# A third shifted copy moves from VectorE to GpSimd in a one-core attention block

## The chip, the cores and the metric

The kernel runs on one core of a Trainium2 chip. A core has five engines, each with an instruction queue that is worked off in order: TensorE (PE) multiplies matrices from SBUF into PSUM, VectorE (DVE) and ScalarE (ACT) work element by element and reach both memories, GpSimd (POOL) works element by element on SBUF alone, and SyncE (SP) issues DMA transfers. Engines wait for each other by semaphores. The metric is the device time of one execution in microseconds (us). Before the change it is 412.21 us, the median of 3 runs (412.16 to 412.69).

## The reference

`x` has 2048 rows of 448. The first half is attention with 16 heads of 28 that share one key and one value projection; the second is an expert layer that only the 8 best rows enter.

```python
h = x + A(layernorm(x))          # A: multi-query attention
def A(x):
    q = (x @ wq) as 16 heads;  k = x @ wk;  v = x @ wv
    p = softmax(q k^T * 28 ** -0.5);  return (p v) @ wo
out = h + B(layernorm(h))
def B(x):
    r = x @ w_r;  idx = argsort(-r)[:8];  s = x[idx]
    y = (silu(s @ w_gate) * (s @ w_up)) @ w_down * sigmoid(r[idx])
    return x + (y added at rows idx)
```

## The kernel before, in words

**Tiles and blocks.** Scores are made transposed: 128 keys by 512 queries. A *block* is one group of four heads (g = b % 4) and one chunk of 512 queries (qb = b // 4), so there are 16 blocks of 16 key tiles j. A tile has scores for four heads: two units p of two matmuls each, two PSUM banks per unit. The score comes out of the multiplication already scaled and offset so that, read as the bits of a bf16 number, it approximates its own exponential.

**Two ways to the exponential.** Most tiles go through ScalarE (`act_unit`): one instruction per unit reads two banks and writes exp to `P` (L845). Others go through VectorE (`dve_unit`, L858): it clamps and converts the PSUM scores to 16-bit integers, which are the bits of a rough exponential `Y[..., 0, ...]`. `shift` (L864) makes three further copies of a tile, each with a constant added to the integers. `dve_pv` multiplies the four copies with four differently scaled copies of the values (`Vs`), and their sum is a better exponential. So a VectorE tile costs VectorE four conversions and three shifts, and TensorE 16 value matmuls in place of 4. `where` and `groups` say which tiles of a block go this way: four, three in blocks 5, 9 and 13, four in the last block, five in all in blocks 0 and 1. Scores of ScalarE's tiles lie in PSUM banks 0 to 3, of VectorE's in 4 and 5; banks 6 and 7 hold the sums of the even and odd blocks, and between two uses such a bank is lent to a projection (`misc_bank`). `Y` has three buffers.

**After a block** (`post_block`) VectorE copies the sums out (`Ot`, L636). The denominators go through DRAM to be spread over 128 partitions (`Lc`), VectorE updates their running minimum and maximum (L640, L642), which serve a check at the end, and takes the reciprocal (L645); a further pair of transfers broadcasts it (`Rb`) and GpSimd multiplies (`On`, L648). After four blocks `out_proj` projects the 512 rows, adds `x`, normalizes (mean and variance on VectorE, the power -1/2 on GpSimd, L670), writes the output row (L677) and the normalized row (L680), and forms the routing score r (L683, L686). Both rows are stored to DRAM, 512 rows at a time.

**The search.** The first 1536 scores r are brought into one row through three transfers, and VectorE finds the eight best and their places (`first_row`, `first_max`; L707, L713, L715). `second_top` turns the places into row numbers and gathers those rows of the output and of the normalized rows by two indirect transfers on GpSimd's queue (L735). The last 512 rows join at the end.

**The order.** Every operation is entered into a graph with a planned duration, what it reads and writes, and a priority, which is mostly a time in units of a sixteenth of a block. `_Graph.plan` simulates the engines and fixes the order of each queue: at each step it starts the ready operation of lowest priority number. On the chip the order is fixed, and the times are not.

## Time and profile before

| | |
|---|---|
| median of 3 runs | 412.21 us |
| time of the profiled execution | 414.31 us |
| its span, first to last instruction | 412.2 us |
| ScalarE busy | 381.1 us, 92% |
| VectorE busy | 366.0 us, 89% |
| TensorE busy | 352.7 us, 86% |
| GpSimd busy | 51.3 us, 12% |

A group's row names line, engine, operation, output and inputs with shapes, the count, then busy time and mean duration in ns, then the idle time just ahead of them and what ended it. Busy time counts overlapping instructions once, so a group's busy time over its count is less than the mean duration. TensorE's work all stands under one helper line, L351, and is told apart by its operands. In a timeline a row has start, length, engine, line and operation, with like neighbours merged. In a row of stretches each engine has its busy time and, in brackets, its number of instructions; the granted TensorE clock, the DMA share and GB/s stand last.

### The profile page before, as it was taken

How to read it: one execution, taken by the hardware profiler on the slowest of the kernel's cores; microseconds unless marked ns; L12 is line 12 of the kernel's file. 1: busy time of each engine (PE TensorE's matmuls, PEld its weight loads, DVE VectorE, ACT ScalarE, POOL GpSimd, SP SyncE). 2: the span in 40 equal slices, each digit the busy share in tenths (PEclk: the TensorE clock that was granted, in tenths of full speed). 3: DMA queues.
4: the chain of work that ended last, by engine and by line, in shares of the span. 5: the costliest groups of instructions: out<-in, count | busy, mean ns of one | idle time of the engine just before them, and what ended most of it. 6: DMA issues, size and time to landing. Idle time of an engine off the chain costs nothing.

```text
span 412.2 us, 8124 instructions
## 1 busy us (share of the span) xinstructions
PE 352.7 (86%) x3335; PEld 110.9 (27%) x3335; DVE 366.0 (89%) x785; ACT 381.1 (92%) x429; POOL 51.3 (12%) x76
## 2 busy tenths in 40 slices
PE   8899989898897998888798997988888987898845
PEld 7333222222221221222122222222222221222235
DVE  5998899999899998989999999889989998998281
ACT  4899998999999999999999999999999999999640
POOL 7231000101010020101000120101010130213000
PEclk9999999999999998999999999999999999999955
DMA  7696000100000002000000002000000002001000
GB/s 197 161 228 160 1 2 4 53 4 28 1 28 0 26 6 91 28 3 26 2 27 2 22 8 92 28 2 29 4 27 2 29 0 94 27 4 29 2 34 18
DMA packets 17845, 15.74 MB, mean 38 GB/s; under 512 B 6440, under 2 KB 14924, under 8 KB 17804
## 3 DMA queue, kind: packets, MB, share of 16 engines
q1 hardware_dynamic: 17708, 15.16, 13.4%
q8 instruction: 27, 0.44, 0.5%
q14 instruction: 14, 0.11, 0.1%
q0 software_dynamic: 96, 0.02, 0.0%
HBM read 11.70 MB, written 3.47 MB: 37 GB/s over the span
## 4 chain that ended last, share of the span: by engine, by line
ACT 54%; PE 27%; DVE 16%; issue 1%; DMA 1%; POOL 0%; SPq 0%; POOLq 0%; DVEq 0%
ACT P L845 53%; PE ps L351 27%; DVE Y L858 7%; DVE Y L864 6%; DVE Ot L636 1%; DMA Lc<-l_scr 1%; DVE bn L772 1%; ACT K L527 0%; DVE idx L972 0%; ACT xn L789 0%; POOL out_dram L1038 0%; DVE On L630 0%; SPq L365 0%; DVE wq_sb L1037 0%; DVE ra L778 0%
## 5 line engine op out<-in xcount | busy, mean ns | idle before, releaser
L845 ACT ACTIVATE P<-ps 128x1024 bf16<-128x1024 f32 x396 | 368.1, 1089 | 6.3 <-PE ps L351 4.3
L351 PE MATMUL ps<-Q,K 64*128 64x512 bf16 x1024 | 183.0, 386 | 42.1 <-ACT P L845 29.5
L858 DVE TENSOR_SCALAR Y<-ps 128x512 int16<-128x512 f32 x232 | 149.5, 680 | 13.2 <-PE ps L351 12.7
L864 DVE TENSOR_SCALAR Y<-Y 128x2048 int16<-128x2048 int16 x174 | 119.0, 715 | 1.5
L351 PEld LDWEIGHTS ps<-Q,K 64*128 64x128 bf16 x1024 | 43.9, 93 | 188.2 <-ACT P L845 146.8
L351 PE MATMUL ps<-P,Vs 128*32 128x512 bf16 x792 | 78.4, 390 | 0.0
L351 PE MATMUL ps<-Y,Vs 128*32 128x512 bf16 x928 | 77.7, 382 | 0.1
L648 POOL TENSOR_TENSOR On<-Ot,Rb 128x512 bf16<-128x512 f32 x15 | 22.4, 1496 | 235.9 <-DMA Rb<-l_scr 235.9
L351 PEld LDWEIGHTS ps<-P,Vs 128*32 128x32 bf16 x792 | 20.1, 93 | 46.1 <-issue 45.5
L351 PEld LDWEIGHTS ps<-Y,Vs 128*32 128x32 bf16 x928 | 23.6, 95 | 24.5 <-issue 12.4
L351 PE MATMUL ps<-xnT,wq_pad 112*128 112x512 bf16 (+1 forms) x68 | 19.3, 377 | 1.4 <-DVE Ot L636 1.2
L351 PE MATMUL ps<-wo_pad,On 128*128 128x448 bf16 (+1 forms) x64 | 17.8, 358 | 2.6 <-DVE Ot L636 1.8
L670 POOL TENSOR_TENSOR st<-st,nhalf 128x1 f32<-128x1 f32 x12 | 9.3, 773 | 65.2 <-DVE st L668 65.2
L466 DVE TENSOR_SCALAR Q<-ps,qone 128x512 bf16<-128x512 f32 x15 | 10.8, 722 | 2.4 <-PE ps L351 2.4
L636 DVE COPY Ot<-ps 128x512 f32<-128x512 f32 x15 | 10.3, 686 | 1.0 <-PE ps L351 0.6
L351 PE MATMUL ps<-ident 128*128 128x128 bf16 x72 | 7.6, 287 | 1.8 <-POOL ident L380 1.8
L683 DVE SCALAR_TENSOR_TENSOR junk<-hbuf,st,w_rb 128x448 bf16<-128x448 f32 x12 | 8.1, 677 | 0.0
L664 DVE TENSOR_TENSOR hbuf<-ps,x_sb 128x448 f32<-128x448 f32 x12 | 7.4, 616 | 0.6 <-PE ps L351 0.6
L666 DVE BATCH_NORM_STATS2 bn<-hbuf 128x6 f32<-128x448 f32 x12 | 7.4, 620 | 0.1
L351 PEld LDWEIGHTS ps<-ident 128*128 128x128 bf16 x72 | 6.9, 134 | 1.8 <-POOL ident L380 1.8
L351 PEld LDWEIGHTS ps<-wo_pad,On 128*128 128x128 bf16 x64 | 4.2, 97 | 11.8 <-issue 7.9
L351 PEld LDWEIGHTS ps<-xnT,wq_pad 112*128 112x128 bf16 x68 | 4.4, 98 | 10.2 <-issue 4.2
(175 smaller groups left out, 171.9 us busy)
## 6 DMA issues: line engine op xcount, KB each, us to landing
Rb<-l_scr SPq DMA_DIRECT2D x15, 256.0 KB
wg_sb<-in_B_w_gate_dram SPq DMA_DIRECT2D x1, 1568.0 KB, 12.7
wu_sb<-in_B_w_up_dram SPq DMA_DIRECT2D x1, 1568.0 KB, 19.6
wd_sb<-in_B_w_down_dram SPq DMA_DIRECT2D x1, 1568.0 KB, 23.3
x_sb<-in_A_x_dram SPq DMA_DIRECT2D x3, 448.0 KB, 6.2
out_dram<-x_sb SPq DMA_DIRECT2D x3, 448.0 KB, 3.1
xn_scr<-xn SPq DMA_DIRECT2D x3, 448.0 KB, 4.0
x_sb<-in_A_x_dram SPq DMA_DIRECT2D x4, 112.0 KB, 2.1
```

The costliest lines, as they stand in the source:

```text
L351: return lambda e: e.matmul(o, lhsT=l, rhs=r, start=start, stop=stop)
L466: G.op(DV, lambda e: e.tensor_scalar(Q[:, b % 4, :], ps[:, bank, :], qone[:, 0:1], None, ALU.add), dvt(512), reads=[pk(bank), "qone"], wri ...
L636: G.op(DV, lambda e: e.tensor_copy(Ot[:, rb, :], ps[:, acc_bank(b), :]), dvt(512), reads=[pk(acc_bank(b))], writes=[("Ot", rb)], prio=u - 30)
L648: G.op(PO, lambda e: e.tensor_tensor(On[:, qb % 2, g, :], Ot[:, rb, :], Rb[:, rb, :], ALU.mult), 1270, reads=[("Ot", rb), ("Rb", rb)], wri ...
L664: G.op(DV, lambda e: e.tensor_tensor(hbuf[:, hr, :], ps[:, bank, 0:D], x_sb[:, t, 0:D], ALU.add), dvt(D), reads=[pk(bank), ("x", t)], writ ...
L666: G.op(DV, lambda e: e.bn_stats(bn6[:, t, :], hbuf[:, hr, :]), dvt(D), reads=[("h", hr)], writes=[("bn6", t)])
L670: G.op(PO, lambda e: e.tensor_tensor(st[:, t, 4:5], st[:, t, 7:8], nhalf[:, 0:1], ALU.pow), 570, reads=[("st7", t), "nhalf"], writes=[("st ...
L683: G.op(DV, lambda e: e.scalar_tensor_tensor(junk[:, :], hbuf[:, hr, :], st[:, t, 4:5], w_rb[:, :], ALU.mult, ALU.mult, accum_out=st[:, t, ...
L772: G.op(DV, lambda e: e.bn_stats(bn6[:, t, :], ps[:, bank, 0:D]), dvt(D), reads=[pk(bank)], writes=[("bn6", t)])
L845: G.op(AC, lambda e: e.activation(P[:, sl, :, :], ps[:, b0:b0 + 2, :], ACT.Exp, bias=EBIAS, scale=OCT), 905, reads=[pk(b0), pk(b0 + 1)], w ...
L858: G.op(DV, lambda e, k=k: e.tensor_scalar(Y[:, n, 0, p + 2 * k, :].bitcast(I16), ps[:, 4 + k, :], 0.0, 32639.0 - 3 * STEP, ALU.max, ALU.mi ...
L864: G.op(DV, lambda e: e.tensor_scalar(Y[:, n, v, :, :].bitcast(I16), Y[:, n, 0, :, :].bitcast(I16), v * STEP, None, ALU.add), 610, reads=[( ...
```

## The change

*Third shift.* From block 2 on, the shift v = 3 of a VectorE tile is made by GpSimd, after VectorE's shifts v = 1 and 2 of the same tile. The planner enters 2030 ns for it, and gets a `lock`: operations of GpSimd and VectorE's shifts exclude each other in the plan. The value matmuls of these tiles get later priorities.

*Tiles.* Blocks 2, 3, 5, 6, 8, 9, 11, 12 and 14 have four VectorE tiles, blocks 4, 7, 10 and 13 five. *Conversions.* One instruction converts both banks of a unit.

*Layer norm.* `out_proj` of the first two row chunks goes one tile to a block in four blocks, that of the third two tiles to each of two blocks. The normalized row is no longer written; the row before normalization is stored in float32 with its two factors beside it, a tile at a time (`hbuf` is 450 wide), and the eight gathered rows are normalized after the gather. Output rows are stored 256 at a time. *Check.* The minimum and maximum of the denominators become sums of them and of their reciprocals, made by GpSimd except in the last block.

*Search.* Two levels: the eight best of each of 12 rows of 128, with their places, and the eight best of those 96; the places go through a table in DRAM, broadcast back to eight partitions, from which a compare picks.

```diff
+        o.lock = (lock or eng == PO) and not dma
@@ plan
+        port = 0.0
...
+                for o in lst:
+                    if o.lock and o.ready < port:
+                        o.ready = port
...
+            if c.lock:
+                port = c.end
@@ post_block
+        LE = DV if b == NB - 1 else PO
-        G.op(DV, lambda e: e.tensor_tensor(Lmn[:, :], Lmn[:, :], Lc[:, rb, :], ALU.min), 85,
-        G.op(DV, lambda e: e.tensor_tensor(Lmx[:, :], Lmx[:, :], Lc[:, rb, :], ALU.max), 85,
+        G.op(DV, lambda e: e.reciprocal(Li[:, rb, :], Lc[:, rb, :]), 170, reads=[("Lc", rb)], writes=[("Li", rb)])
...
+        G.op(LE, lambda e: e.tensor_tensor(Lsi[:, :], Lsi[:, :], Li[:, rb, :], ALU.add), 150,
+        G.op(LE, lambda e: e.tensor_tensor(Ls[:, :], Ls[:, :], Lc[:, rb, :], ALU.add), 150,
@@ out_proj
+    def ln_block(qb, k):
+        return 4 * qb + 5 + (k if qb < 2 else k // 2)
-        G.op(DV, lambda e: e.tensor_scalar(xn[:, t, :], hbuf[:, hr, :], st[:, t, 4:5], st[:, t, 6:7],
-                                           ALU.mult, ALU.add), 420,
...
+        dma(xs[t * 128:(t + 1) * 128, :], hbuf[:, hr, :], [("xs", t)], reads=[("h", hr), ("h4", hr), ("h6", hr)],
+            lat=3000.0)
+        if k % 2:
+            evs.append(dma(out_v[:, t - 1:t + 1, :], outf[:, t - 1:t + 1, :], [("out", qb, k)],
@@ first_row, first_max
-        G.op(DV, lambda e: e.tensor_copy(r12[:, :], ps[0:12, bank, 0:128]), 200, reads=[pk(bank)], writes=["r12"])
+        G.op(DV, lambda e: e.max(top12[:, :], ps[0:12, bank, 0:128]), 220, reads=[pk(bank)], writes=["top12"])
+        G.op(DV, lambda e: e.max_index(idx12[:, :], top12[:, :], ps[0:12, bank, 0:128]), 300,
+        G.op(DV, lambda e: e.tensor_scalar(pos12[:, :], idx12[:, :], p128[0:12, 0:1], None, ALU.add), 90,
+        dma(v_row[0:1, :].rearrange("o (t k) -> o t k", k=8), top12[:, :], ["v_row"], reads=["top12"])
+        dma(ptab[0:96].rearrange("(t k) -> t k", k=8), pos12[:, :], ["ptab"], reads=["pos12"])
+        dma(prow[:, :], ptab.partition_broadcast(8), ["prow"], reads=["ptab"])
-        G.op(DV, lambda e: e.max(top8[:, 0, :], r_row[:, :]), 1700, reads=[("r_row", c) for c in range(3)],
-        G.op(DV, lambda e: e.max_index(idx8[:, 0, :], top8[:, 0, :], r_row[:, :]), 1760,
+        G.op(DV, lambda e: e.max(top8[:, 0, :], v_row[:, :]), 180, reads=["v_row"], writes=[("top8", 0)])
+        G.op(DV, lambda e: e.max_index(idx8[:, 0, :], top8[:, 0, :], v_row[:, :]), 260,
@@ second_top
+        G.op(DV, lambda e: e.tensor_copy(sel3[:, :], ps[0:8, bank, 0:1]), 70, reads=[pk(bank)], writes=["qsel"])
+        G.op(DV, lambda e: e.scalar_tensor_tensor(ohq[:, :], iota96[:, :], sel3[:, 0:1], prow[:, :], ALU.is_equal,
+                                                  ALU.mult, accum_out=posc[:, :]), 220,
...
+        G.op(DV, lambda e: e.tensor_scalar(xnc[:, 0:D], hc[:, 0:D], hc[:, D:D + 1], hc[:, D + 1:D + 2], ALU.mult,
+                                           ALU.add), 420, reads=["hc"] + old, writes=["xnc"])
@@ tiles
-    groups = [4] * NB
-    for b in range(5, NB, 4):
-        groups[b] = 3
+    groups = [0, 4, 4, 4, 5, 4, 4, 5, 4, 4, 5, 4, 4, 5, 4, 4]
@@ dve_unit, shift
-        for k in range(2):
-            G.op(DV, lambda e, k=k: e.tensor_scalar(Y[:, n, 0, p + 2 * k, :].bitcast(I16), ps[:, 4 + k, :], 0.0,
-                                                    32639.0 - 3 * STEP, ALU.max, ALU.min), 610, reads=[pk(4 + k)],
+        G.op(DV, lambda e: e.tensor_scalar(Y[:, n, 0, p:p + 3:2, :].bitcast(I16), ps[:, 4:6, :], 0.0,
+                                           32639.0 - 3 * STEP, ALU.max, ALU.min), 1140, reads=[pk(4), pk(5)],
...
+        po = v == 3 and b > 1
+        G.op(PO if po else DV, lambda e: e.tensor_scalar(Y[:, n, v, :, :].bitcast(I16), Y[:, n, 0, :, :].bitcast(I16),
+                                                             v * STEP, None, ALU.add), 2030 if po else 605,
+             reads=[("Y", n, 0, 0), ("Y", n, 0, 1)] + ([("Y", n, 1), ("Y", n, 2)] if po else []),
+             writes=[("Y", n, v)], lock=True)
@@ priorities
-            pv_list.append((t + 2.2 + 0.5 * v, dve_pv, m, v, b, j))
+            pv_list.append((t + (4.2 if b > 1 else 2.2) + 0.5 * v + (1.5 if v == 3 and b > 1 else 0), dve_pv, m, v, b, j))
-                    at(16 * b + 37.5 + k * 2.0, out_proj, b // 4, k)
+                    at(16 * ln_block(b // 4, k) + (9.5 if b < 11 else 4.5 + 6.0 * (k % 2)), out_proj, b // 4, k)
-    at(16 * 14 + 5.0, first_top)
-    at(16 * 14 + 9.0, first_max)
+    at(16 * 14 + 14.0, first_top)
+    at(16 * 15 + 1.0, first_max)
-    at(16 * 2 + 2.5, q_project, 3, misc_bank(2))
+    at(16 * 2 + 5.0, q_project, 3, misc_bank(2))
```

More of the change, by code (lines that the diff above doesn't have):

```diff
@@ L750, in last_w @@
                                                            ALU.mult, ALU.mult, accum_out=xw[:, k:k + 1]), 600,
-                 reads=[("x", 12 + k), "w_rb"], writes=["junk", ("xw", k)])
+                 reads=[("x", 12 + k), "w_rb", ("scr0", 3)], writes=["junk", ("xw", k)])
     LB = (4, 5, 6, 0)
@@ L871, in dve_pv @@
                   for i in range(4)], 216,
[L872 removed]
+             reads=([("Y", n, v)] if v else [("Y", n, 0, 0), ("Y", n, 0, 1)]) + [("V", j // 4), "V1"],
+             writes=[pk(acc_bank(b))], form=2)
     for n, (b, j, t) in enumerate(act_tiles):
@@ L1039, in _main @@
                                                 fin[:, :], None), 1000, dma=True,
-             reads=["fin", "idxc"] + [("out", q) for q in range(3)] + [("out", 3, 1), ("out", 3, 3)],
+             reads=["fin", "idxc"] + [("out", q, k) for q in range(4) for k in (1, 3)],
              writes=[("out", 4)])
```

135 lines of the change are left out of this document (71 added, 64 removed).

## The prediction

> **What bounds the kernel now.** I read the page first: busy shares, the chain, the costliest groups.
>
> ```profile
> span 412.2 us, 8124 instructions
> PE 352.7 (86%) x3335; PEld 110.9 (27%) x3335; DVE 366.0 (89%) x785; ACT 381.1 (92%) x429; POOL 51.3 (12%) x76
> ACT P L845 53%; PE ps L351 27%; DVE Y L858 7%; DVE Y L864 6%; DVE Ot L636 1%; DMA Lc<-l_scr 1%; DVE bn L772 1%; ACT K L527 0%; DVE idx L972 0%; ACT xn L789 0%; POOL out_dram L1038 0%; DVE On L630 0%; SPq L365 0%; DVE wq_sb L1037 0%; DVE ra L778 0%
> L845 ACT ACTIVATE P<-ps 128x1024 bf16<-128x1024 f32 x396 | 368.1, 1089 | 6.3 <-PE ps L351 4.3
> L858 DVE TENSOR_SCALAR Y<-ps 128x512 int16<-128x512 f32 x232 | 149.5, 680 | 13.2 <-PE ps L351 12.7
> L864 DVE TENSOR_SCALAR Y<-Y 128x2048 int16<-128x2048 int16 x174 | 119.0, 715 | 1.5
> ```
>
> ScalarE is 92% busy and one line of it, the exponentials (L845), carries 53% of the chain; VectorE, at 89%, is close behind. The shares are averages, so I next cut the span into stages (busy time by engine: TensorE, its weight loads, VectorE, ScalarE, GpSimd), and asked the line view of L845 where its train begins and ends.
>
> ```profile
> 0.00:62.00 62.00, 53.94 (x524) 24.57 (x525) 53.76 (x135) 54.60 (x65) 15.80 (x46) 1.00 0.51 124
> 62.00:365.00 303.00, 265.45 (x2397) 71.08 (x2395) 284.50 (x561) 297.49 (x321) 30.08 (x26) 0.99 0.08 24
> 387.00:412.00 25.00, 13.03 (x240) 9.73 (x236) 12.70 (x60) 7.84 (x22) 0.93 (x1) 0.62 0.07 22
> L845 ACT ACTIVATE P<-ps x396: 1018/1072/1283, 12.4 to 385.2; 128x1024 bf16<-128x1024 f32 x198
> ```
>
> From 62 to 365 us, which is blocks 2 to 14, ScalarE works 297.5 of 303 us on 321 exponentials: 0.927 us each, and 5.5 us idle. VectorE works 284.5 us, so 18.5 us of slack. Fewer exponentials shorten this stage as long as VectorE, TensorE and what the two share with GpSimd follow. The 25 us after 387 hold no exponential and belong to the last projection and the expert layer.
>
> **The change, part by part.**
>
> *Seven tiles from ScalarE to VectorE.* The list of VectorE tiles per block goes from 4, with 3 in blocks 5, 9 and 13, to 4, with 5 in blocks 4, 7, 10 and 13: 49 become 56 in blocks 2 to 14; the first five and the last four stay. Each tile is two exponentials: 14 x 0.927 = **13.0 us** less on ScalarE.
>
> *VectorE's tile.* A tile was four conversions and three shifts. By the groups, 149.5/232 = 0.644 and 119.0/174 = 0.684 us each: 4.63 us. It becomes two conversions of 1024 columns and, from block 2 on, two shifts. No row has such a conversion; the searches below give the pace of one element:
>
> ```profile
> L713 DVE MAX8 top<-xnT 1x8 f32<-1x1536 f32 x1 | 1.7, 1732 | 0.0
> L715 DVE FIND_INDEX8 idx<-top,xnT 1x8 uint32<-1x1536 f32 x1 | 1.7, 1739 | 0.0
> L971 DVE MAX8 top<-ps 1x8 f32<-1x520 f32 x1 | 0.7, 689 | 0.0
> L707 DVE COPY r<-ps 12x128 f32<-12x128 f32 x1 | 0.3, 279 | 0.1
> L680 DVE TENSOR_SCALAR xn<-hbuf,st 128x448 bf16<-128x448 f32 x12 | 6.1, 506 | 0.0
> L677 DVE TENSOR_SCALAR x_sb<-hbuf,st 128x448 bf16<-128x448 f32 x12 | 6.1, 508 | 0.0
> L683 DVE SCALAR_TENSOR_TENSOR junk<-hbuf,st,w_rb 128x448 bf16<-128x448 f32 x12 | 8.1, 677 | 0.0
> L640 DVE TENSOR_TENSOR Lmn<-Lmn,Lc 128x16 f32<-128x16 f32 x16 | 2.7, 166 | 2.6 <-DMA Lc<-l_scr 2.5
> L642 DVE TENSOR_TENSOR Lmx<-Lmx,Lc 128x16 f32<-128x16 f32 x16 | 2.7, 167 | 0.0
> ```
>
> (1732 - 689)/1016 = 1.03 ns an element, so 512 more columns add 0.53 us: 1.17 us, between 0.68 us (no dearer than one bank) and 1.29 us (nothing saved). I take 1.17. The new tile is 2 x 1.17 + 2 x 0.684 = 3.71 us. In blocks 2 to 14: 56 x 3.71 - 49 x 4.63 = 207.8 - 226.9 = -19.1 us.
>
> *Other VectorE work.* The store of the normalized row (L680) goes: -6.1 us. The two running bounds (L640, L642) become sums on GpSimd, except in the last block: 15 x 0.333 = -5.0 us. The search over 1536 (L707, L713, L715: 3.75 us) becomes eleven short ones, eight-best over 12 rows of 128, then over 96, a pick from a table, and the scaling of eight gathered rows: by L707 for the short ones and L680 for the scaling some 2 us, so -1.7 us. VectorE in the stage: 284.5 - 19.1 - 6.1 - 5.0 - 1.7 = 252.6 us, against ScalarE's 297.5 - 13.0 = 284.5.
>
> *The third shift on GpSimd.* 60 of them, 56 in the stage. Its price is the largest unknown. GpSimd's rows:
>
> ```profile
> L583 POOL TENSOR_SCALAR xn<-x_sb,nmean,rstd 128x448 bf16<-128x448 bf16 x5 | 3.5, 716 | 0.3
> L398 POOL MEMSET wq_pad<- 128x2048 bf16 x1 | 1.8, 1794 | 0.0
> L433 POOL CAST iota_n<-iota_i 128x5 f32<-128x5 int32 x1 | 0.3, 257 | 0.0
> L648 POOL TENSOR_TENSOR On<-Ot,Rb 128x512 bf16<-128x512 f32 x15 | 22.4, 1496 | 235.9 <-DMA Rb<-l_scr 235.9
> ```
>
> Nearest is L583, the same operation on two-byte data: with L433's 0.257 us as the fixed part, (0.716 - 0.257)/448 = 1.02 ns an element, so 0.26 + 2048 x 1.02 ns = **2.36 us**. Ends: 1.79 (a write of as many elements, L398) and 3.27 (L583 scaled whole). The planner enters 2.03.
>
> *The port.* Two places in the timeline show that a VectorE shift and a GpSimd operation exclude each other:
>
> ```profile
> 285.34 1.28 DVE L858 TENSOR_SCALAR Y<-ps 128x512 int16<-128x512 f32 x2
> 286.54 1.73 DVE L864 TENSOR_SCALAR Y<-Y 128x2048 int16<-128x2048 int16 x2
> 375.92 1.28 DVE L864 TENSOR_SCALAR Y<-Y 128x2048 int16<-128x2048 int16 x2
> 285.84 1.27 POOL L648 TENSOR_TENSOR On<-Ot,Rb 128x512 bf16<-128x512 f32 x1 [21.11 <-DMA Rb<-l_scr]
> 240.94 0.68 DVE L683 SCALAR_TENSOR_TENSOR junk<-hbuf,st,w_rb 128x448 bf16<-128x448 f32 x1
> 239.87 0.54 POOL L670 TENSOR_TENSOR st<-st,nhalf 128x1 f32<-128x1 f32 x1
> 240.97 1.11 POOL L670 TENSOR_TENSOR st<-st,nhalf 128x1 f32<-128x1 f32 x1 [0.56 <-DVE st L668]
> ```
>
> GpSimd held from 285.84 to 287.11; two conversions beside it ran at their usual 1.28, but the two shifts from 286.54 took 1.73 instead of the 1.28 of those at 375.92: the first waited for GpSimd's end. The other way round, the power at 240.97 took 1.11 us, not the 0.54 of the one at 239.87, behind L683, which reads two tensors from SBUF. The Trainium skill ("SBUF — State Buffer", Who interferes with whom) states this as an exclusive lock held for a whole instruction, the loser fully blocked; the rows agree.
>
> So the stage has a second budget, the port: GpSimd's old work 30.1 us, 26 sums at about 0.25 us (L433) 6.5, its shifts 56 x 2.36 = 132; VectorE's shifts 112 x 0.684 = 77, L683 8.1 and L677 6.1. That is 260 us of the some 290 that remain: 90%. It fits because GpSimd's shift waits for VectorE's two of that tile, after which VectorE has 2.34 us of conversions, which do not touch the port. What does not fit: some 0.2 us a tile of start delay and excess, 56 x 0.2 = 11 us; and L683 and L677, which the planner does not count as port users: 24 starts x 45% (GpSimd's share of the time) x half of 2.36 us = 13 us. VectorE then needs 252.6 + 24 = 277 us, 97% of ScalarE's 284.5, where before it was 96%. I leave ScalarE's 5.5 us of idle and add **2 us** for the tighter fit (bounds -5.5, all idle gone, and +17, from the rival below).
>
> *TensorE.* A moved tile has three further groups of four value matmuls.
>
> ```profile
> L351 PE MATMUL ps<-Y,Vs 128*32 128x512 bf16 x928 | 77.7, 382 | 0.1
> 273.00:295.00 22.00, 19.51 (x182) 1.00 0.05 14
> ```
>
> 77.7/232 = 0.335 us a group: 7 x 3 x 0.335 = 7 us, in a stage with 303 - 265 = 37 idle: 0 (bounds 0 and +4, a rival). Spreading layer-norm tiles over more blocks moves work, and adds none.
>
> *Queues.* SP issues 18 stores for 12 rows' tiles instead of 6.
>
> ```profile
> SPq L365 <- DVE x_sb L677: 31.1, 2, 16.0
> xnT<-out_dram,idc POOLq DMA_INDIRECT x1, 2.7
> xnT<-xn_scr,idc POOLq DMA_INDIRECT x1, 5.8
> 369.43 1.35 POOL L735 DMA_INDIRECT xnT<-out_dram,idc  x1 [10.30 <-DVE idc L727]
> 371.09 1.63 POOL L735 DMA_INDIRECT xnT<-xn_scr,idc  x1 [0.30 <-issue]
> ```
>
> SP already stood 16.0 us behind one layer-norm output with block chains behind it, and On was still in time; GpSimd's shifts now queue behind On's multiplication, which waits for that chain. I take 0 (bounds 0 and +8). The scaling of gathered rows is a new wait on VectorE: the planner gives the two gathers 4 us, the trace 371.09 + 5.8 - 369.43 = 7.5 from the first. So VectorE may stand up to 3.5 us, with the last block's shifts, and the matmuls that read them, queued behind it. I take **+1 us** (bounds 0 and +3.5). At the end two sums and a reciprocal replace three small operations, and two flag operations go: 0, within 0.3 us.
>
> **Sum.** 412.2 - 13.0 + 2 + 1 = 402.2 us of span. The profiled execution took 414.31 us for that span, but the median of the runs shown, 412.21, equals the span, so I forecast **402 us**, 2.5% faster.
>
> **The rivals.**
>
> *B, VectorE's relief also takes the stalls away.* VectorE's waits for TensorE (12.7 us at L858) and ScalarE's idle shrink: 412.2 - 13.0 - 5 = 394 to 397, say 396. For it: VectorE's 32 us of relief. Against: the port.
>
> *C, slower: the port becomes the bound.* With a shift of 3.27 us the port's sum is 128 + 183 = 311 us, more than the 303 of the stage now; with some 3% lost at each hand-over 320, so 412 + 17 = 429. It decides from (303 - 128)/56 = 3.13 us. For it: the ends above, and that the order is fixed by planned times, so that any drift puts a shift behind GpSimd. Against: L398 and L583's slope. At On's pace per element (1.27/512 = 2.5 ns) a shift is 5.1 us and the time beyond 500. The Trainium skill speaks for a slow one ("GPSIMD Engine Reference", Elementwise: some 2.6 cycles an element at 1.2 GHz, an estimate of 4.4 us from that page), though it puts that down to two inputs; L648, with two inputs, is near that pace and L583, with one, is not.
>
> *D, GpSimd's queue.* On late by its DMA chain holds a shift, its value matmuls, and the block's end: +8 us, 410.
>
> *E, TensorE limits the five-tile blocks.* Such a block has 22 exponentials, 20.4 us; the block from 273 to 295 shows TensorE 19.5 us busy, plus 1.0 for the fifth tile: level. One us in each of four blocks: 406. Against: busy time counts modelled ends.
>
> **How the numbers follow.** The forecast 0.48, B 0.12, C 0.20, D 0.10, E 0.10. What this measurement tells from no change is about 0.2%, 0.8 us. The forecast, B, E and half of D, which spreads about its 410, are faster: 0.75; 0.03 of D is the same; C and the last 0.02 of D are slower: 0.22. The range goes from B's middle, 395, to 416, beyond D; most of C is outside it. Without C the range would be 395 to 411.
>
> **What would show it.** L845 x382 at about 0.93 us; ScalarE's idle in the long stage near 7 us; 60 GpSimd shifts near 2.4 us; conversions x130 near 1.2 us; VectorE's shifts near 0.69 us with few above 1 us. A mean shift on VectorE over 0.9 us, or GpSimd over 3 us, makes it wrong by C; On ahead of long waits on GpSimd by D; ScalarE waiting for TensorE in blocks 4, 7, 10 and 13 alone by E; a wait of VectorE for the gather over 3 us spoils the +1.

## The result and the profile after

The changed kernel takes **561.57 us** (561.1 to 562.59, 6 runs) against 412.19 us (6 runs) of the kernel before: 1.3614 times as long, with an interval of 1.3581 to 1.3647. The forecast was 402.0 us, with a range of 395 to 416. So it was wrong by 160 us and in sign. The profiled execution took 562.59 us for a span of 560.8 us.

The page of the changed kernel first: span, busy shares, the chain by engine and by line, and the groups that answer to those shown of before (L876 was L845, L888 was L858, L895 was L864).

```profile
span 560.8 us, 8228 instructions
PE 405.7 (72%) x3419; PEld 114.5 (20%) x3419; DVE 488.6 (87%) x607; ACT 379.5 (68%) x415; POOL 389.8 (70%) x172
...
DVE 58%; PE 20%; POOL 11%; ACT 8%; issue 3%; POOLq 0%; DVEq 0%
DVE Y L895 23%; PE ps L368 20%; DVE Y L888 18%; POOL Y L895 9%; ACT P L876 7%; DVE hbuf L701 5%; DVE x_sb L703 2%; DVE junk L705 1%; DVE Q L487 1%; DVE wo_pad L777 1%; DVE hbuf L691 1%; DVE bn L693 1%; DVE xnT L762 1%; DVE x_sb L708 1%; DVE Ot L658 1%
...
L876 ACT ACTIVATE P<-ps 128x1024 bf16<-128x1024 f32 x382 | 366.5, 1034 | 152.5 <-PE ps L368 151.1
L895 POOL TENSOR_SCALAR Y<-Y 128x2048 int16<-128x2048 int16 x60 | 322.8, 5380 | 85.1 <-DVE Y L895 74.7
...
L895 DVE TENSOR_SCALAR Y<-Y 128x2048 int16<-128x2048 int16 x135 | 192.8, 1454 | 0.6
L888 DVE TENSOR_SCALAR Y<-ps 128x1024 int16<-128x1024 f32 x130 | 158.9, 1222 | 23.5 <-PE ps L368 23.1
...
L701 DVE SCALAR_TENSOR_TENSOR hbuf<-mv,hbuf 128x1 f32<-128x1 f32 x12 | 28.9, 2410 | 0.0
```

ScalarE, 92% busy before, is now 68% busy and stood idle 152.5 us ahead of its exponentials, waiting for scores. The chain runs over VectorE (58%), where exponentials carried 53% of it before. Two rows explain that. GpSimd's shift takes 5380 ns, where the forecast had 2360. VectorE's own shift takes 1454 ns on average, where it took 715: the two signs that the prediction named for its rival C (over 3 us, over 0.9 us). The line view of L895 shows that VectorE's shift has not become slower work:

```profile
L895 DVE TENSOR_SCALAR Y<-Y x135: 623/684/4832, 42.6 to 520.8; 128x2048 int16<-128x2048 int16 x135
L895 POOL TENSOR_SCALAR Y<-Y x60: 5365/5366/5671, 69.6 to 528.9; 128x2048 int16<-128x2048 int16 x60
```

The three durations are the least, the median and the longest. The median shift of VectorE is 684 ns (685 before), and the longest 4832 ns: some of them stand for most of a GpSimd shift. The timeline from 200 us shows how (start, length, engine):

```profile
200.01 5.37 POOL L895 TENSOR_SCALAR Y<-Y 128x2048 int16<-128x2048 int16 x1 [1.23 <-DVE Y L895]
206.60 5.37 POOL L895 TENSOR_SCALAR Y<-Y 128x2048 int16<-128x2048 int16 x1 [1.22 <-DVE Y L895]
202.71 3.81 DVE L895 TENSOR_SCALAR Y<-Y 128x2048 int16<-128x2048 int16 x2
209.31 3.20 DVE L895 TENSOR_SCALAR Y<-Y 128x2048 int16<-128x2048 int16 x1
```

GpSimd's shift holds the port from 200.01 to 205.38. Two shifts of VectorE come up at 202.71; the first waits until 205.38, and both are done at 206.52. GpSimd's next shift starts only then, at 206.60: it waits for VectorE's shifts, since the change puts it behind them. At 209.31 the same happens again. The two engines hand the port back and forth, and no shift of the one runs beside a shift of the other. Only VectorE's conversions do, such as one from 201.58 to 202.79. The long stage (busy time of TensorE, its weight loads, VectorE, ScalarE, GpSimd, then the granted clock) gives the sum:

```profile
62.00:515.00 453.00, 322.85 (x2543) 75.90 (x2541) 413.69 (x431) 305.73 (x318) 353.80 (x114) 0.83 0.06 19
```

GpSimd holds the port for up to 353.8 us; VectorE's shifts need about 112 x 0.684 = 77 us of it, L705 and L703 (formerly L683 and L677) about 8 and 6. That is at most 445 of 453 us, since GpSimd's figure holds its own waits for the port too: in this stage the port is the bound.

### The profile page after: what moved, and what is told of

The parts are those of the page before. It is cut to its first block, busy times and chain, and to the rows that moved or that the text cites. A ratio compares the mean times of both kernels' runs of the same rounds, so it can differ in the third digit from the quotient of the medians.

```text
span 560.8 us, 8228 instructions
## 1 busy us (share of the span) xinstructions
PE 405.7 (72%) x3419; PEld 114.5 (20%) x3419; DVE 488.6 (87%) x607; ACT 379.5 (68%) x415; POOL 389.8 (70%) x172
## 4 chain that ended last, share of the span: by engine, by line
DVE 58%; PE 20%; POOL 11%; ACT 8%; issue 3%; POOLq 0%; DVEq 0%
DVE Y L895 23%; PE ps L368 20%; DVE Y L888 18%; POOL Y L895 9%; ACT P L876 7%; DVE hbuf L701 5%; DVE x_sb L703 2%; DVE junk L705 1%; DVE Q L487 1%; DVE wo_pad L777 1%; DVE hbuf L691 1%; DVE bn L693 1%; DVE xnT L762 1%; DVE x_sb L708 1%; DVE Ot L658 1%
## 5 line engine op out<-in xcount | busy, mean ns | idle before, releaser
L876 ACT ACTIVATE P<-ps 128x1024 bf16<-128x1024 f32 x382 | 366.5, 1034 | 152.5 <-PE ps L368 151.1
L895 POOL TENSOR_SCALAR Y<-Y 128x2048 int16<-128x2048 int16 x60 | 322.8, 5380 | 85.1 <-DVE Y L895 74.7
L368 PE MATMUL ps<-Q,K 64*128 64x512 bf16 x1024 | 201.6, 437 | 105.9 <-DVE Y L888 93.7
L895 DVE TENSOR_SCALAR Y<-Y 128x2048 int16<-128x2048 int16 x135 | 192.8, 1454 | 0.6
L888 DVE TENSOR_SCALAR Y<-ps 128x1024 int16<-128x1024 f32 x130 | 158.9, 1222 | 23.5 <-PE ps L368 23.1
L368 PE MATMUL ps<-Y,Vs 128*32 128x512 bf16 x1040 | 107.0, 452 | 25.9 <-POOL Y L895 24.9
L368 PEld LDWEIGHTS ps<-Y,Vs 128*32 128x32 bf16 x1040 | 26.7, 101 | 68.0 <-POOL Y L895 30.1
L667 POOL TENSOR_TENSOR Ls<-Ls,Lc 128x16 f32<-128x16 f32 x15 | 8.2, 549 | 39.0 <-DMA Lc<-h_scr 39.0
L701 DVE SCALAR_TENSOR_TENSOR hbuf<-mv,hbuf 128x1 f32<-128x1 f32 x12 | 28.9, 2410 | 0.0
L703 DVE TENSOR_SCALAR x_sb<-hbuf,st 128x448 bf16<-128x448 f32 x12 | 14.4, 1204 | 0.0
L697 POOL TENSOR_TENSOR hbuf<-st,nhalf 128x1 f32<-128x1 f32 x12 | 10.2, 850 | 1.4 <-DVE st L695 1.4
L665 POOL TENSOR_TENSOR Lsi<-Lsi,Li 128x16 f32<-128x16 f32 x15 | 7.6, 504 | 5.1 <-DVE Li L662 3.6
```

Of the source, the lines that this page charges most:

```text
L368: return lambda e: e.matmul(o, lhsT=l, rhs=r, start=start, stop=stop)
L665: G.op(LE, lambda e: e.tensor_tensor(Lsi[:, :], Lsi[:, :], Li[:, rb, :], ALU.add), 150, reads=["Lsi", ("Li", rb)], writes=["Lsi"])
L667: G.op(LE, lambda e: e.tensor_tensor(Ls[:, :], Ls[:, :], Lc[:, rb, :], ALU.add), 150, reads=["Ls", ("Lc", rb)], writes=["Ls"])
L697: G.op(PO, lambda e: e.tensor_tensor(s4, st[:, t, 7:8], nhalf[:, 0:1], ALU.pow), 570, reads=[("st7", t), "nhalf"], writes=[("h4", hr)])
L701: G.op(DV, lambda e: e.scalar_tensor_tensor(s6, mv[:, t, 0:1], -1.0, s4, ALU.mult, ALU.mult), 85, reads=[("mv", t), ("h4", hr)], writes=[( ...
L703: G.op(DV, lambda e: e.tensor_scalar(outf[:, t, :], h, st[:, t, 5:6], s6, ALU.mult, ALU.add), 420, reads=[("h", hr), ("st5", t), ("h6", hr ...
```

## The experiments

The theory after the first look: GpSimd's shift costs 5.4 us instead of 2.4 us, and the port, which one engine holds at a time, makes every such microsecond a microsecond of the kernel. Rivals: the shift is slow only because of waits on the port; or the value matmuls that read the late third copy delay the block; or something else in the change (tiles, conversions, the layer norm's order) is to blame.

### The price of the shift on GpSimd alone

GpSimd runs ten forms of the operation, three times each, with nothing beside it.

```diff
+ lambda e: e.tensor_scalar(y_i16[:, :], ai, 96.0, None, ALU.add),             # as in the changed kernel
+ lambda e: e.tensor_scalar(y_bf2[:, :], a[:, :], 1.5, 0.5, ALU.mult, ALU.add),
+ lambda e: e.tensor_copy(y_cp[:, :], ai),
...
```

> Leaves out the whole computation; GpSimd works off ten operations one at a time, three times each, with VectorE idle. Theory 'type': the 5.37 us of the shift comes from its 16-bit integers. Then the 16-bit integer addition on 2048 columns takes 5.4 us with no port user beside it, on 512 columns about 0.26 + 512 x 2.5 ns = 1.5 us, and the same form on bf16 data about 2.4 us. Rival 'length': the pace falls on long rows whatever the type; then bf16 on 2048 columns takes about 5.4 us too, and the integer addition on 512 columns 0.8 us. Rival 'lock': the 5.37 us hold waiting for the port; then the same addition alone takes about 2.4 us. For an exact 32-bit integer addition over 1024 columns, which adds to two 16-bit numbers at once, the pace of the two-input On row (2.5 ns) gives 2.8 us.

The groups of that run, with the mean of one operation in ns:

```profile
L39 POOL TENSOR_SCALAR y_i<-a 128x2048 int16<-128x2048 int16 x3 | 16.1, 5365 | 8.2 <-DVE z L57 8.0
L48 POOL TENSOR_SCALAR y_bi<-a 128x2048 int16<-128x2048 bf16 x3 | 16.1, 5367 | 0.2
L41 POOL TENSOR_SCALAR y_bf<-a 128x2048 bf16<-128x2048 bf16 x3 | 16.1, 5367 | 0.2
L44 POOL TENSOR_SCALAR y_i<-src_i 128x1024 int32<-128x1024 int32 x3 | 8.3, 2775 | 0.2
...
L42 POOL TENSOR_SCALAR y_bf<-a 128x2048 bf16<-128x2048 bf16 x3 | 5.7, 1901 | 0.2
L46 POOL TENSOR_TENSOR y_tb<-src_i,con 128x1024 int32<-128x1024 int32 x3 | 5.7, 1892 | 0.2
L43 POOL COPY y_cp<-a 128x2048 int16<-128x2048 int16 x3 | 5.7, 1893 | 0.2
L40 POOL TENSOR_SCALAR y_half<-a 128x512 int16<-128x512 int16 x3 | 4.5, 1489 | 0.2
```

The shift takes 5365 ns with no VectorE beside it, so waits on the port don't make it long. Type doesn't either: an addition that reads bfloat16 (L48) costs the same as on int16, and 1024 columns of int32 (L44) cost half. Nor is it the addition: one multiplication alone, on bfloat16 (L41), costs the same. A call with **two** steps, multiply and add (L42), takes 1901 ns, as short as a plain copy (L43). Here one step costs more than two. A tensor plus one broadcast column in int32 (L46) is fast as well.

> Leaves out the whole computation; eight forms on GpSimd alone, one at a time, three times each. Theory 'form': any two steps are fast whatever they are (add-add, multiply-add, add-min, with constants or with per-partition scalars: 1.9 to 2.5 us on 2048 columns), any single step slow (5.4 us), and on 1024 and 512 columns add-add takes about 1.1 and 0.7 us. Rival 'multiply': add-add and add-min take 5.4 us and only the forms with a multiply first are fast.

A second list of forms asked what the fast ones have in common (L43 adds twice, L44 multiplies and adds, L45 adds and takes a minimum, L47 adds and multiplies with the numbers from a tensor):

```profile
L43 POOL TENSOR_SCALAR y_half<-a 128x2048 int16<-128x2048 int16 x3 | 21.3, 7090 | 0.2
L45 POOL TENSOR_SCALAR y_bi<-a 128x2048 int16<-128x2048 int16 x3 | 21.2, 7081 | 0.2
...
L47 POOL TENSOR_SCALAR y_bf<-a,pf 128x2048 bf16<-128x2048 bf16 x3 | 6.1, 2048 | 0.3
...
L44 POOL TENSOR_SCALAR y_cp<-a 128x2048 int16<-128x2048 int16 x3 | 5.7, 1900 | 0.2
```

Add-add and add-minimum take 7.1 us, so two steps as such are not fast, and neither expectation held: they are dearer than one step. Of the forms tried, the pairs of one multiplication and one addition are, at 0.9 to 1.0 ns a column; one step costs 2.6 ns and the other pairs 3.5 ns.

### The third shift back on VectorE

```diff
-        po = v == 3 and b > 1
+        po = False
```

> The changed kernel with the third shift back on VectorE and nothing else undone. Theory 'price': GpSimd's 5.37 us on the port is the whole loss; VectorE then needs 252.6 + 56 x 0.684 = 291 us in the long stage against ScalarE's 284.5, so VectorE bounds it and the time is 405 to 415 us. Rival 'rest': another part (layer norm spread over blocks, the search, five-tile blocks, priorities) costs as well; then the time stays above 425 us.

Measured: 405.89 us (405.67 to 406.25), 0.9833 of before (0.9815 to 0.9852). The loss is gone with this one line, and the rest of the change gains 1.7%, in the order that the plan then gives. VectorE is then full:

```profile
62.00:355.00 293.00, 264.16 (x2441) 71.49 (x2437) 287.34 (x459) 284.07 (x307) 35.82 (x54) 1.00 0.09 28
```

### Is it the port, or the late copy?

In the first of two runs the shift stays at 5.38 us, but the value matmuls read the second copy, so that no matmul waits for the third; by the trace this moves some of TensorE's matmuls to other places in the order. In the second run the shift is the dearer add-add of the same numbers, in the order of the changed kernel.

```diff
-            Y[:, n, v, i, :], f, l)
+            Y[:, n, min(v, 2) if b > 1 else v, i, :], f, l)
```

> The changed kernel with GpSimd's shift as it is, 5.37 us, but the value matmuls of the third copy read the second copy instead from block 2 on, so that nothing but the reuse of the buffer waits for GpSimd; the third copy is left out of the sums. Theory 'port': VectorE's own shifts wait for the port, so the time stays above 530 us. Rival 'lateness': TensorE waits for late third copies, and without that the time falls below 450 us.

```diff
-            v * STEP, None, ALU.add)
+            v * STEP, 0.0 if po else None, ALU.add, *([ALU.add] if po else []))
```

> The changed kernel with the third shift still on GpSimd and the same numbers, but written with two arithmetic steps (add 96, add 0) in place of one. On GpSimd alone the one-step forms took 5.37 us for 2048 columns on 16-bit integers and on bf16 alike, and the one two-step form 1.90. Theory 'form': the shift falls to about 1.9 us, VectorE's shifts stop waiting, and the time is 396 to 402 us, as with the memset. Rival 'multiply': only the pair multiply-add is fast; then the shift stays at 5.4 us and the time above 550 us.

The unread copy: 555.69 us in one run, 6 us under the changed kernel. The add-add: 664.33 us (663.74 to 665.11), 1.6096 of before (1.6053 to 1.6139). The rows of L895, of the first and of the second:

```profile
L895 POOL TENSOR_SCALAR Y<-Y 128x2048 int16<-128x2048 int16 x60 | 323.1, 5385 | 80.5 <-DVE Y L895 73.9
...
L895 DVE TENSOR_SCALAR Y<-Y 128x2048 int16<-128x2048 int16 x135 | 190.5, 1437 | 0.6
```

```profile
L895 POOL TENSOR_SCALAR Y<-Y 128x2048 int16<-128x2048 int16 x60 | 425.9, 7098 | 85.4 <-DVE Y L895 75.0
...
L895 DVE TENSOR_SCALAR Y<-Y 128x2048 int16<-128x2048 int16 x135 | 261.1, 1959 | 0.6
```

With nobody reading the copy, VectorE's shifts are as long (1437 ns) and the time nearly the same: the late copy is not the cause. The second run was expected at 396 to 402 us, before the list of forms had shown what add-add costs. Its 60 shifts are 7.098 - 5.380 = 1.718 us longer and should cost 103 us if all of it is in series; 664.33 - 561.57 = 102.8 us were measured.

### The same order with a cheaper operation

Five runs leave the operation on GpSimd and put another form in the place of the slow one: an int32 addition of a broadcast column to pairs of 16-bit numbers, entered in the plan at 2300 ns and again at 2030 ns as in the changed kernel; a one-step int32 addition of 2.8 us; a memset; and a multiplication by 1 with the addition, which gives the same numbers. Apart from the run with 2300 ns, the planned durations and, by the traces, the order of every engine's instructions are those of the changed kernel. The code is shortened here.

```diff
-        G.op(PO if po else DV, lambda e: e.tensor_scalar(Y3, Y0, v * STEP, None, ALU.add), 2030 if po else 605,
+        e.tensor_tensor(Y3_int32, Y0_int32, c3[:, 0:1].broadcast_to([128, 1024]), ALU.add)   # 2300, then 2030
+        e.tensor_scalar(Y3_int32, Y0_int32, 96.0, None, ALU.add)
+        e.memset(Y3, 1.0)
+        e.tensor_scalar(Y3, Y0, 1.0, v * STEP, ALU.mult, ALU.add)
```

> The changed kernel with the third shift still on GpSimd, but as an exact 32-bit integer addition of 96 x 65537 over 1024 columns, planned at 2.3 us. Theory 'price': with 2.3 to 2.8 us per shift the port's sum is 128 + 56 x 2.3 = 257 to 285 us of the stage, and the time is 400 to 412 us. Rival 'plan': an order fixed by planned times cannot keep two port users apart on the chip; then VectorE's shifts still wait often, and the time is above 420 us even with the short operation.

> The 32-bit form of the third shift (measured 1.9 us), entered in the plan with 2.03 us, the figure of the changed kernel, in place of 2.3. Nothing else differs. Theory 'order': the 413.67 us of the first 32-bit kernel came from the order that the longer figure gave; the time falls to 403 us or less. Rival 'reads': the form itself costs, since it reads SBUF through two inputs while VectorE's two-input operations wait for that; then the time stays at 409 us or more.

> The changed kernel with the third shift as one addition over 1024 32-bit columns, which takes 2.77 us alone; its numbers are not exact, so the third copy is off by rounding. Theory 'port in series': each microsecond of the operation counts 60 times, as between 5.37 and 7.10 us (664.33 - 561.57 = 102.8 for 60 x 1.73), down to ScalarE's floor: 561.6 - 60 x 2.60 = 406 us. Rival 'hidden until 3.13 us', the point worked out in the prediction: 402 us or less.

> The changed kernel with GpSimd's shift replaced by a memset of the same tile, so the third copy is wrong: the constant stands in place of the shifted scores. The memset takes 1.8 us (1.79 for as many elements before). Theory 'price': 398 to 403 us, the forecast with the shortest price. Rival 'plan': above 415 us.

> The changed kernel with the third shift on GpSimd written as multiply by 1, add 96, which gives the same numbers and took 1.90 us alone, against 5.37 for the single addition. The order of every queue is that of the changed kernel. Theory 'form': the choice of the arithmetic steps is the whole loss; VectorE's shifts wait no more than they did in the kernel before, and the time is 396 to 402 us, below both kernels and below the 405.89 with the shift on VectorE. Rival 'plan': reading SBUF brings back waits that the memset did not have; 404 us or more.

| operation on GpSimd | one, us | time, us | ratio to before |
|---|---|---|---|
| memset | 1.81 | 398.04 (one run) | |
| int32 with a column, planned 2030 | 1.90 | 406.69 | 0.9848 (0.9823 to 0.9874) |
| multiply and add | 1.91 | 407.70 | 0.9875 (0.9841 to 0.9909) |
| int32 with a column, planned 2300 | 1.96 | 413.67 | 1.0007 (0.9984 to 1.003) |
| int32, one addition | 2.82 | 413.26 (one run) | |
| one addition (the changed kernel) | 5.38 | 561.57 | 1.3614 |
| add, add | 7.10 | 664.33 | 1.6096 |

From 2.82 to 5.38 us the time rises by 148.3 us, 58 for each microsecond of the shift; beyond, by 60. Carried back from 5.38 at 60 a microsecond, the line meets 407.7 us at 2.8 us: above that every one of the 60 counts nearly in full. Below it the shift is hidden for the most part: from 1.91 to 2.82 us the time rises by 5.6 us (the 2.82 is one run, and neither of its expectations, 406 and at most 402, held). And the planned duration alone, 2300 or 2030 ns for the same operation, is worth 7 us, by the order it makes.

So multiplying by 1 in the same call, which changes no number and no order, takes 154 us off the changed kernel. The rows of L895 in the multiply-and-add kernel:

```profile
L895 POOL TENSOR_SCALAR Y<-Y 128x2048 int16<-128x2048 int16 x60 | 114.5, 1908 | 128.3 <-DVE Y L895 97.8
...
L895 DVE TENSOR_SCALAR Y<-Y 128x2048 int16<-128x2048 int16 x135 | 91.8, 706 | 0.6
```

VectorE's shifts are back at 706 ns. VectorE as a whole is busy 355.4 us where it was 488.6. It does the same work in both, so 133 us of the 154 were its own instructions standing, 101 of them its shifts (192.8 - 91.8). My expectation for the time, 396 to 402, was missed; what the rest is comes below.

### Two parts alone

The multiply-and-add kernel with the old list of tiles, and (second diff) the kernel before with the conversions over two banks as its only change:

```diff
-    groups = [0, 4, 4, 4, 5, 4, 4, 5, 4, 4, 5, 4, 4, 5, 4, 4]
+    groups = [4] * NB
+    for b in range(5, NB, 4):
+        groups[b] = 3
```

```diff
-        for k in range(2):
-            ... ps[:, 4 + k, :] ...
+        G.op(DV, lambda e: e.tensor_scalar(Y[:, n, 0, p:p + 3:2, :].bitcast(I16), ps[:, 4:6, :], 0.0,
```

> The multiply-add kernel with the tile list of the kernel before (three VectorE tiles in blocks 5, 9 and 13, four in the others), so 14 exponentials return to ScalarE. Theory 'ScalarE bounds': 14 x 0.93 = 13 us more than the multiply-add kernel, 409 to 415 us. Rival 'balanced': VectorE or TensorE set the pace as much, and the time rises by less than 5 us.

> The kernel before with the conversions over two banks and nothing else. VectorE saves 2 x (1.29 - 1.17) = 0.24 us a tile, 14 us in all. Theory 'ScalarE bounds the kernel before': little of it reaches the end, 408 to 412.5 us. Rival 'VectorE bounds it': 398 to 404 us.

With the old tiles: 416.42 us (413.42 to 417.67), 1.0097 of before (1.0064 to 1.0131). The seven tiles are worth 416.42 - 407.70 = 8.7 us, not 13, between the two expectations. Some 2.3 of the 8.7 lie outside the span: with the old tiles the time is 4.0 to 4.2 us above the span, in the multiply-and-add kernel 1.8 to 1.9, and the runs do not show why. The conversions alone: 413.49 us, 1.0021 (1.0001 to 1.0041), no gain, although VectorE's busy time falls from 366.0 to 358.2 us. The likely reason is that this time was not on the path before; the other planned duration changes the order as well, and no run separates the two.

### Where the rest of the forecast went

The stage of the multiply-and-add kernel that answers to the forecast's, and then its last block in the timeline:

```profile
62.00:355.00 293.00, 267.31 (x2466) 73.14 (x2464) 273.21 (x405) 285.54 (x308) 143.24 (x110) 0.99 0.09 28
```

```profile
367.18 3.42 POOL L766 DMA_INDIRECT xnT<-out_dram,idc  x1 [0.23 <-issue]
370.91 0.86 POOL L766 DMA_INDIRECT xnT<-h_scr,idc  x1 [0.30 <-issue]
371.80 1.27 POOL L671 TENSOR_TENSOR On<-Ot,Rb 128x512 bf16<-128x512 f32 x1
373.03 3.76 POOL L895 TENSOR_SCALAR Y<-Y 128x2048 int16<-128x2048 int16 x2
368.02 2.48 DVE L895 TENSOR_SCALAR Y<-Y 128x2048 int16<-128x2048 int16 x4
373.26 3.78 DVE L769 TENSOR_SCALAR xnT<-xnT 8x448 bf16<-8x448 f32 x1 [2.77 <-DMA xnT<-h_scr,idc]
```

The first gather's issue takes 3.42 us on GpSimd beside four shifts of VectorE. Behind it stand the other gather, On, and the last two third shifts, which start at 373.03. VectorE stands 2.77 us for the gather and then 3.78 us in an operation on eight rows (L769), which ends with GpSimd's shifts. Three runs took this apart, on top of the multiply-and-add kernel: L769 put behind the copy of the last block's sums; that, and the last block's third shifts on VectorE; and the first edit with all third shifts on VectorE. A fourth run makes the third copy a plain copy on GpSimd, in the order of the changed kernel.

```diff
+    def scale_rows():                       # L769, now behind the last block's first copy of sums
+        ... reads=["hc", ("OtH", 1)] + old, writes=["xnc"], prio=290)
-        po = v == 3 and b > 1
+        po = v == 3 and 1 < b < 15          # second run
```

```diff
-            ... e.tensor_scalar(Y3, Y0, v * STEP, None, ALU.add)
+            ... e.tensor_copy(Y3, Y0)           # fourth run
```

> The multiply-and-add form (1.90 us) as before, but the scaling of the gathered rows stands behind VectorE's first copy of the last block's sums instead of ahead of it. The trace of the multiply-and-add kernel has VectorE standing 2.77 us for the gather and 3.78 us in the scaling, while the last two GpSimd shifts end at 376.8. Theory 'the scaling on VectorE is the place': some 3 us less, 403 to 405.5. Rival 'the last shifts on GpSimd are the place': VectorE's wait goes but the sums still wait for those two shifts, 406.5 to 408.5.

> As the run beside it, and the four third shifts of the last block are made by VectorE. In the trace of the multiply-and-add kernel the last two started at 373.03, behind the gather (3.42 us of issue) and On. Theory 'the last block's queue on GpSimd': another 2 to 4 us less, 400 to 403.5. Rival 'spread over the stage': within 1 us of the run beside it.

> All third shifts on VectorE (405.89 us before), the scaling of the gathered rows moved as above. Theory 'the scaling's wait is on the path': 403 to 405 us. Rival 'the last block's path is the value matmuls, and the wait is beside them': 405.5 to 406.5.

> The third shift is a plain copy of the tile on GpSimd (1.89 us in the run of prices), so the third copy of the scores is not shifted and the output is not the reference's; order and waits are those of the changed kernel. Theory 'an operation that reads SBUF holds up VectorE's two-input and four-tensor work': as with multiply and add, 405.5 to 410. Rival 'the memset's gain was its shorter time or chance': 397 to 402.

L769 late alone: 406.89 us (405.66 to 408.21), 0.8 us less, which is within the scatter of the two kernels. With the last block's shifts on VectorE: **403.63 us** (402.4 to 405.6), another 3.3 us less, 0.977 of before (0.9734 to 0.9805). With all shifts on VectorE: 406.29 us, no different from 405.89. The 406.89 us and the 403.63 us kernels have nearly one order, and their traces part in the last block: the 361st of the 382 exponentials starts 0.6 us sooner, the last one 2.8 us sooner in the latter. So what held the end was GpSimd's queue in the last block, and VectorE's wait for the gather was mostly beside it. The timeline of the second run shows the queue without the shifts:

```profile
365.69 1.15 POOL L766 DMA_INDIRECT xnT<-out_dram,idc  x1 [3.46 <-DVE idc L756]
367.14 0.91 POOL L766 DMA_INDIRECT xnT<-h_scr,idc  x1 [0.30 <-issue]
368.07 1.28 POOL L671 TENSOR_TENSOR On<-Ot,Rb 128x512 bf16<-128x512 f32 x1
```

The copy took 1902 ns and the kernel 406.17 us (405.64 to 406.7), 0.9828 of before (0.9789 to 0.9867): as with the multiplication, and 8 us over the memset, although the two runs have one order. The groups, of the copy and then of the memset:

```profile
L897 POOL COPY Y<-Y 128x2048 bf16<-128x2048 bf16 x60 | 114.1, 1902 | 127.5 <-DVE Y L900 101.7
...
L701 DVE SCALAR_TENSOR_TENSOR hbuf<-mv,hbuf 128x1 f32<-128x1 f32 x12 | 10.9, 910 | 0.0
L705 DVE SCALAR_TENSOR_TENSOR junk<-hbuf,w_rb 128x448 bf16<-128x448 f32 x12 | 10.3, 856 | 0.0
```

```profile
L897 POOL MEMSET Y<- 128x2048 bf16 x60 | 108.3, 1805 | 128.9 <-DVE Y L900 102.4
...
L705 DVE SCALAR_TENSOR_TENSOR junk<-hbuf,w_rb 128x448 bf16<-128x448 f32 x12 | 8.1, 675 | 0.0
...
L701 DVE SCALAR_TENSOR_TENSOR hbuf<-mv,hbuf 128x1 f32<-128x1 f32 x12 | 3.6, 297 | 0.0
```

L701 and L705 read two tensors from SBUF. Beside an operation of GpSimd that reads SBUF they stand for 613 and 181 ns more each than beside one that only writes. The Trainium skill ("SBUF — State Buffer", Who interferes with whom) states this rule: a VectorE instruction with two SBUF inputs contends with a GpSimd instruction that reads SBUF, not with one that only writes it. The two traces agree. In the memset's, eight of the twelve L701 started in the middle of a memset and took 144 to 150 ns, and three fell on On, which reads SBUF, and took 734 to 761. In the copy's, eight started in the middle of a copy, and each ended with it.

The two traces also show where the 8 us lie. With the memset the 61st exponential starts 0.8 us sooner, the 361st 4.7 us and the last one 8.5 us. So about 3.9 us come in the long stage, where L701 and L705 stand 9.5 us less, and 3.8 us in the last block. There the first gather's issue began 0.92 us ahead of VectorE's four shifts with the memset and took 1.15 us; with the copy it began 0.85 us ahead of them and took 3.43 us.

### Do these two operations, or the order, hold the rest?

On top of the 403.63 us kernel, one run enters L701 and L705 in the plan as users of the port; the control enters GpSimd's shift at 1930 ns instead of 2030, the same work in another order.

```diff
-             reads=[("mv", t), ("h4", hr)], writes=[("h6", hr)])
+             reads=[("mv", t), ("h4", hr)], writes=[("h6", hr)], lock=True)
```

```diff
-            ... 2030 if po else 605,
+            ... 1930 if po else 605,
```

> As the run with the last block's shifts on VectorE (403.63 us), with L701 and L705 (the two operations of the normalization that read two tensors from SBUF) entered in the plan as users of the port. In that run L701 took 905 ns instead of 297 beside writes alone, L705 858 instead of 675: 9.5 us in all on VectorE. Theory 'unplanned port users are the rest': both fall back near 300 and 680 and the time to 398 to 401.5. Rival 'the order, not these operations': 402 to 406, whatever the two take.

> As the run with the last block's shifts on VectorE (403.63 us), with GpSimd's shift entered in the plan at 1930 ns instead of 2030 (it takes 1.90 us on the chip). The same work in another order. If the order alone moves the time by several us, this differs from 403.6 by more than 2 us to either side; if not, 402.5 to 405.

With the lock: 407.89 us (407.45 to 408.75), slower by 4.3 us and outside both expectations, although the two operations now wait for nothing. Its rows:

```profile
L892 DVE TENSOR_SCALAR Y<-ps 128x1024 int16<-128x1024 f32 x130 | 158.3, 1218 | 27.6 <-PE ps L368 27.0
...
L705 DVE SCALAR_TENSOR_TENSOR junk<-hbuf,w_rb 128x448 bf16<-128x448 f32 x12 | 8.2, 679 | 0.0
...
L701 DVE SCALAR_TENSOR_TENSOR hbuf<-mv,hbuf 128x1 f32<-128x1 f32 x12 | 1.8, 150 | 0.0
```

VectorE gained 11 us in them and lost most of it waiting for scores: 27.0 us ahead of its conversions, where the kernel under it stood 17.4. But the lock also moved more than half of VectorE's instructions to other places in its queue. The control: **401.79 us** (401.1 to 402.94), 0.9736 of before (0.9709 to 0.9763). It is the fastest version here that computes the reference, faster than both kernels; in it ScalarE stands only 5.8 us for scores:

```profile
L880 ACT ACTIVATE P<-ps 128x1024 bf16<-128x1024 f32 x382 | 354.3, 1087 | 6.8 <-PE ps L368 5.8
```

So taking the two operations' waits away by the plan does not pay here. What the waits cost by themselves these two runs do not show; the copy and the memset, in one order, leave room for some 3.9 us. The lock changed waits and order together. The control, too, changed both: L705 is back at 0.67 us in it without any lock, and L701 at 0.77. Its 1.8 us are less than the 2 us set for it, and its interval overlaps that of the 403.63 us kernel, so that an order alone moves the time is shown by the 7 us between 2300 and 2030 ns, and by this control hardly. The memset's run is 3.8 us faster than the control; it has another order, it is one run, and its operation is 0.1 us shorter and reads nothing, and no run separates these.

## Why the prediction was wrong

**The step that failed** is "The third shift on GpSimd": "Nearest is L583, the same operation on two-byte data". It is not the same operation. L583 adds and multiplies in one call; the shift only adds. A multiply-and-add of 2048 columns takes 1.90 us, and an add-and-multiply with its numbers from a tensor, the form of L583, 2.05: less than what L583's slope gave (2.36) and inside the ends. The addition alone takes 5.37 us, outside the upper end of 3.27. The line view of before has rows of GpSimd with a single step, a comparison:

```profile
L380 POOL TENSOR_SCALAR ident<-idi 128x128 bf16<-128x128 int32 x1 | 0.6, 563 | 0.0
L442 POOL TENSOR_SCALAR sel<-idi 128x128 f32<-128x128 int32 x1 | 0.6, 557 | 0.0
```

With L433's 257 ns as the fixed part, they give (563 - 257)/128 = 2.4 ns an element, so 0.26 + 2048 x 2.4 ns = 5.2 us for the shift. I passed over them because their elements are four bytes wide, and took the row whose data type matched instead of the one whose steps matched.

**The port.** The model was right. "It decides from (303 - 128)/56 = 3.13 us" came out near 2.8 us, with 5.6 us lost already at 2.82. GpSimd's share of it was right too but for the price: 30.1 + 6.5 + 56 x 1.91 = 143.6 us, and 143.2 in the multiply-and-add kernel. Rival C, whose remark on On's pace gave "5.1 us and the time beyond 500", is what happened: 5.38 us a shift and 561.57 us. By its sum the stage would have taken 128 + 56 x 5.38 = 429 us; it took 453, so that some 0.4 us were lost with each shift. Its main case, 429 us at 3.27 us a shift, was the mildest of it, and its 0.20 came from a price range that did not hold L380.

**The rule set aside.** The Trainium skill ("GPSIMD Engine Reference", Elementwise — side-by-side cycle accounting) gave an estimate of 4.4 us, nearer to the 5.37 us than my 2.36. I set it aside because it speaks of two inputs, and On, with two, was near that pace. Its pace, by that estimate 2.2 ns a column, fits neither form of the scalar operation here: the one-step shift is slower, at 2.6 ns a column, and the multiply-and-add, with as many inputs, far faster, at 0.93.

**The other terms** are tested by the multiply-and-add kernel, which differs from the changed one in this price alone:

- *VectorE's work and ScalarE's.* Forecast 277 us and 284.5 us in the stage, with 7.5 us idle on ScalarE; measured 273.2 and 285.5 in 293 us, 7.5 idle. The conversion, 1.17 us, measured 1.22. The +2 us for the tighter fit held.
- *Seven tiles, -13.0 us.* The exponentials saved are 14 x 0.927; undoing them with the rest in place costs 8.7 us, of which some 6.4 lie inside the span. Part of what they free is given back as waits: ScalarE stands 11.2 us ahead of its exponentials in the multiply-and-add kernel and 5.4 with the old tiles.
- *TensorE, 0.* It works 267.3 of 293 us in the stage, about what was counted (265.45 of 303 before, plus 7); whether the blocks of five tiles carry some of the 8.7 us was not tried.
- *The gather wait, +1 us (0 to 3.5).* VectorE stood 2.77 us, but moving L769 gave 0.8 us, within the scatter. What cost more was behind it on GpSimd's own queue, 3.3 us: rival D's mechanism, a shift held in that queue, though by the gather and in the last block alone.
- *Sum.* The last exponential began at 385.2 us before, and at 377.4 in this kernel by its line view:

```profile
L876 ACT ACTIVATE P<-ps x382: 1018/1047/1229, 12.5 to 377.4; 128x1024 bf16<-128x1024 f32 x191
```

  That is 7.8 us earlier instead of the 10.0 of the sum; from there to the end of the span of 406.0 us it is 28.6 us instead of 27.0; and the median lies 1.7 us above that span, which I had set to zero. 402.2 + 2.2 + 1.6 + 1.7 = 407.7, the time measured.

With the last block's queue mended and another planned duration the same change gives 401.79 us. That the number meets the forecast is partly luck: a planned duration alone moved the time by 7 us in one pair of runs.

## What to carry to other kernels

Before work is moved to GpSimd, find a row of it with the *same arithmetic steps*, not only the same instruction name and data type, or measure that form alone: here the pair multiply-and-add cost 1.90 us, the addition alone 5.37 and two additions 7.09. Where two engines share a port and take turns in an order fixed beforehand, add up what each holds it: well inside the period the price is mostly hidden, and beyond it each microsecond counts as often as the operation occurs (here 60 times). And what an engine's queue holds at the end of a kernel (here two shifts behind a gather whose issue grew to 3.4 us) is to be looked at by itself: here it cost 3.3 us.

## What was unexpected of the hardware

- GpSimd's scalar operation is slower with one step than with a multiplication and an addition: 5365 ns against 1901 for 2048 columns of bfloat16 or int16, alone on the engine. Add-add takes 7090, add-minimum 7081, multiply-add 1900, add-multiply with numbers from a tensor 2048, one multiplication alone 5367. Why is not shown by these runs.
- An int32 addition of two tensors of 1024 columns takes 2337 ns on GpSimd, and 1892 where the second is one broadcast column.
- The granted TensorE clock was 0.83 in the long stage of the changed kernel against 0.99 before, while TensorE was less busy (322.85 of 453 us against 265.45 of 303). Over the whole span it was 0.84 and, in the add-add run, 0.79, against 0.97 before. The score matmuls took 437 ns on average in the changed kernel and 387 in the multiply-and-add one. TensorE stood waiting in those stages, so this is taken as a consequence; it was not tested by itself.
- An indirect DMA's issue on GpSimd took 3.42 us where four shifts of VectorE in a row began 0.84 us after it, and 1.15 us in the run with the last block's shifts on VectorE, where one began 0.93 us after it.
